# An attention and gMLP kernel on one core: three x transposes moved to DMA, two gMLP batches begun four slots later, four products open in the tail

## The chip, the cores and the metric

The kernel runs on one core of a Trainium2 chip. The metric is the device time of one execution in microseconds; several runs are summed up by their median. A profile is taken of one execution by the hardware profiler.

## The reference

Block-sparse attention for 4 batches of 8 heads (768 positions, head size 64), then a gMLP block with a spatial gate over each batch's attention output. The parts that matter:

```python
scores = scale * np.matmul(q, k.transpose(0, 1, 3, 2))
scores = np.where(mask, scores, -1000000000.0)
attn = np.exp(scores - np.max(scores, axis=-1, keepdims=True))
attn = attn / (np.sum(attn, axis=-1, keepdims=True) + 1e-09)
attn_out = np.matmul(attn, v)
# heads side by side: x is (4, 768, 512)
h = np.maximum(x @ w_in, 0.0)            # 512 -> 1024
u, v = h[..., :512], h[..., 512:]
v_n = (v - mean(v)) / np.sqrt(var(v) + 1e-06)
v_s = np.einsum('ts,bsd->btd', w_spatial, v_n) + b_spatial[None, :, None]
out = (u * v_s) @ w_out
```

Inputs and output are float32; the kernel multiplies in bf16.

## The kernel before

**Pairs and slots.** Two heads of a batch form a pair, so there are 16 pairs, four for each batch: pairs 4 to 7 are batch 1, 8 to 11 batch 2, 12 to 15 batch 3. The program is written as a list of slots, 0 to 188. Each slot emits one piece of the scores (two matmuls, L471) with its exp on ScalarE (L475), and the product with v (six matmuls, L522) of a piece seven slots older. From slot 36 on pair p has twelve slots from `slot_of(p)` = 36 + 12 (p - 4). Every engine takes its instructions in the order in which they are written; only data and buffers decide when.

**Between the pieces** come gMLP steps. A gMLP batch is 108 steps, each one matmul of 512 columns (L596): 48 for v and u (`in_steps`; a product is four steps, one for each pair of the batch, which needs that pair's transposed x), 36 for the spatial product (`s_product`), 24 for the output (`o_product`). Steps wait in one queue. For batch 0 the table `STEPS` says how many run in which slot; batches 1 and 2 are dealt over 48 slots by `deal` and `run_queue`, 2.25 a slot. Batch 3 comes behind the last slot, in the tail. Its start is `last_x` (slot 188): it first empties the queue.

**x of a pair.** When both heads of a pair are normalized by VectorE (L486 and L487; in the 19th slot of the pair, counted from its first as 0: slot 90 for pair 7), x lies with positions on partitions. The gMLP needs it transposed (`xt`). Pairs whose number leaves a remainder of 0 to 2 by four have that done by a DMA transpose from the SP queue (`xtr_dma`, L553). Pairs 7 and 11 have it done on TensorE (`xtr_pe`: six transposes of 128x128, L289, and a copy on VectorE, L218), and pair 15 the same way inside `last_x`. Batches 1 and 2 begin in the slot in which pair 7 and pair 11 are transposed, 92 and 140.

**The SP queue** carries nearly all DMAs in written order: the loads of q, k, v of a pair 34 slots ahead (L110), the DMA transpose of a pair's q and k (`tr_dma`, L428, `tt<-nat`) 20 slots ahead, x transposes (L553), transposes of the gated product (L678) and stores of the output (L697). An issue waits for its data and for the DMA that stands eight places ahead of it in the queue. VectorE later copies `tt` into place (`split`), five and three slots ahead of the pair.

**PSUM.** A product holds a bank until it is copied out. In the loop the gMLP has two banks (`moeA`, `moeB`); in the tail `moe_ps` turns round six. `last_x` before opens three products of batch 3 with the steps of pairs 12 to 14, transposes x of pair 15 in between, and then closes them.

Of the kernel before, what the change touches and what calls it, by code (L numbers as in the profile page):

```python
# [26 lines left out]
def kernel(  # L27
# [18 lines left out]
    B, H, S, D = q.shape  # L46
# [3 lines left out]
    NCH = S // 128  # L50
# [6 lines left out]
    NG = H // 2  # L57
    NP = B * NG
# [6 lines left out]
    TW = TC * 128  # L65
    S0 = NT * NG * 3
# [150 lines left out]
    def dve_copy(o, i):  # L217
        nc.vector.tensor_copy(out=o, in_=i)  # L218
# [58 lines left out]
    moe_tags, held = deque(["moeA", "moeB"]), set()  # L277

    def moe_tag():
        moe_tags.rotate(1)  # L280
        if moe_tags[0] in held:
            moe_tags.rotate(1)
        return moe_tags[0]

    def bank(nm="ps", tag=None):
        return psum.tile([128, 1024], BF16, tag=tag or moe_tag(), bufs=2 if tag else 1, name=nm)

    def tr(ps, c, in_):
        nc.tensor.transpose(out=ps[:, c * 128:(c + 1) * 128], in_=in_, identity=ident)  # L289

    def pair_of(src, c):
        return src[:, c].rearrange("p h d -> p (h d)")
# [142 lines left out]
    a_ref, av_ref, x_ref, xn_ref, xt_ref = {}, {}, {}, {}, {}  # L435
# [96 lines left out]
    def xt_tile(p):  # L532
        if p not in xt_ref:
            xt_ref[p] = work.tile([128, S], BF16, tag="xt", bufs=7, name="xt")
        return xt_ref[p]

    def xtr_pe(p, xn, c0, n, ps=None):
        if ps is None:
            ps = bank()
        for c in range(n):  # L540
            tr(ps, c, pair_of(xn, c))
        dve_copy(xt_tile(p)[:, c0 * 128:(c0 + n) * 128], ps[:, 0:n * 128])
# [180 lines left out]
    def deal(steps, slots):  # L723
        queue.extend(steps)
        pace["slots"], pace["credit"] = slots, 0.0

    def run_queue(n=None):
        if n is not None:
            for _ in range(n):
                queue.popleft()()  # L730
            return
        if not queue or pace["slots"] <= 0:
            return
        pace["credit"] += (len(queue) - pace["credit"]) / pace["slots"]
        pace["slots"] -= 1
        n = int(pace["credit"] + 0.5)
        for _ in range(min(n, len(queue))):
            queue.popleft()()
            pace["credit"] -= 1
# [5 lines left out]
    def when(slot, *fns):  # L745
        at.setdefault(slot, []).extend(fns)

    def c(f, *a, **kw):
        return lambda: f(*a, **kw)
# [19 lines left out]
    def moe_begin(b):  # L769
        moe[b] = Moe(b)  # L770
# [19 lines left out]
    when(18, lambda: first["steps"].popleft()())  # L790
    when(20, close_first)
    when(29, lambda: deal(moe[0].in_steps("v2 v3 u2 u3", TC), 14))
    STEPS = {20: 0, 21: 3, 22: 2, 23: 0, 24: 2, 25: 1, 26: 2, 27: 2, 28: 0, 29: 1, 30: 1, 31: 1, 32: 2, 33: 1, 34: 1, 35: 1, 36: 1, 37: 0, 38: 1, 39: 2, 40: 2, 41: 2, 42: 1, 43: 3, 44: 3, 45: 0, 46: 2, 47: 1, 48: 2, 49: 1, 50: 2, 51: 0, 52: 2, 53: 1, 54: 1, 55: 1, 56: 2, 57: 3, 58: 1, 59: 1, 60: 2, 61: 2, 62: 3, 63: 1, 64: 1, 65: 1, 66: 1, 67: 2, 68: 3, 69: 1, 70: 1, 71: 1, 72: 1, 73: 2, 74: 2, 75: 1, 76: 1, 77: 3, 78: 1, 79: 1, 80: 1, 81: 2, 82: 0, 83: 3, 84: 1, 85: 2, 86: 0, 87: 2, 88: 2, 89: 3, 90: 2, 91: 0}
    when(42, lambda: deal(moe[0].in_steps("v4 v5 u4 u5", TC) + moe[0].rest_steps(),
                          S0 + 8 + 48 - 42))
    for b in (1, 2):
        s0 = S0 + 48 * b + 8
        when(s0, c(moe_begin, b),
             lambda b=b: deal(moe[b].in_steps(SEQ, 3) + moe[b].rest_steps(), 48))

    last_steps = []


    def last_x():
        moe_begin(B - 1)
        m = moe[B - 1]
        while queue:
            queue.popleft()()
        seq = m.in_steps("v0 v1 u0 v2 v3 v4 v5 u1 u2 u3 u4 u5", 3)
        n = NG - 1  # L810
        for i in (0, 1):
            for f in seq[i * NG:i * NG + n]:
                f()
        ps, xn = bank(), xn_ref.pop(("p", NP - 1))
        moe_tags.rotate(1)
        for cc in range(NCH):
            tr(ps, cc, pair_of(xn, cc))
        xt = xt_tile(NP - 1)
        for cs in (slice(0, TW), slice(TW, S)):
            dve_copy(xt[:, cs], ps[:, cs])  # L820
        for f in seq[2 * NG:2 * NG + n]:
            f()
        for i in (0, 1, 2):
            seq[i * NG + n]()
        last_steps.extend(seq[3 * NG:])

    def slot_of(p):
        return S0 + 12 * (p - NG)

    for p in range(NG, NP):  # L830
        g = slot_of(p)
        when({4: 13, 5: 22, 6: 31}.get(p, g - 34), c(load, p, "k"), c(load, p, "q"), c(load, p, "v"))
        when({4: 18, 5: 26, 6: 38}.get(p, g - 24),
             c(cast, p, "k", PL), c(cast, p, "q", PL), c(cast, p, "v", PL))
        when({4: 20, 5: 31}.get(p, g - 20), c(tr_dma, p))
        when(31 if p == 4 else g - (7 if p in (9, 13) else 5), c(split, p, 0))
        when(32 if p == 4 else g - 3, c(split, p, 1))
        if p == NP - 1:
            when(g + 20, last_x)
        elif p % NG == NG - 1:  # L840
            when(g + 20, lambda p=p: xtr_pe(p, xn_ref.pop(("p", p)), 0, NCH))
        else:
            when(g + 20, c(xtr_dma, p))
    for i, (ld, ca) in enumerate([(16, 19), (16, 21), (17, 23), (17, 25), (18, 27), (18, 29)]):
        when(ld, c(ws_load, i))
        when(ca, c(ws_cast, i))
# [12 lines left out]
    for s in range(NS + LAG + 2):  # L859
# [11 lines left out]
        for f in early:  # L871
            f()
        run_queue(STEPS.get(s))
        for f in late.get(s, []):
# [34 lines left out]
```

## Time and profile before

| | |
|---|---|
| median of 3 runs | 209.66 us (209.59 to 211.54) |
| the profiled execution | 209.93 us |
| its span, first to last instruction | 208.1 us |
| mean granted TensorE clock | 0.998 |
| busy: TensorE, weight loads, VectorE, ScalarE, GpSimd | 200.9, 127.8, 133.1, 168.3, 74.3 us |
| DMA | 41.82 MB, 201 GB/s over the span |

The difference between the execution's time and the span lies ahead of the first and behind the last instruction. Times in the timeline are counted from the span's start. Lengths of matmuls overlap: the start of the next one says how long one held the engine.

### The profile page before, as it was taken

Reading aid. Unit: us, or ns where it says so; the run is one execution under the profiler, and the core shown is the slowest. Engines: PE = TensorE matmul, PEld = TensorE weight load, DVE = VectorE, ACT = ScalarE, POOL = GpSimd, SP = SyncE. Lnnn points to the kernel's source line nnn. Section 1 sums busy time; section 2 is a strip of 40 time slices with the busy share of each in tenths; the row PEclk is TensorE's granted clock in tenths of the full one; section 3 lists DMA queues with packets and bytes.
Section 4 is the critical chain, followed back from the end, with each engine's and each line's share of the span. In section 5 each row is a group of like instructions: output and inputs, shape, how many; then the busy total and the mean of one; then the engine's idle time right before and its main releaser. Section 6 shows DMA issues by size and latency. Waiting matters only on the chain.

```text
span 208.1 us, 5248 instructions
## 1 busy us (share of the span) xinstructions
PE 200.9 (96%) x2106; PEld 127.8 (61%) x2140; DVE 133.1 (64%) x287; ACT 168.3 (81%) x223; POOL 74.3 (36%) x116
## 2 busy tenths in 40 slices
PE   8899999999999999999999999999999999999993
PEld 6689778766666666655655565565556556544441
DVE  7578797989764455594986464385885433567542
ACT  6899999999989889989898888979999787266021
POOL 7998789684681404042064040041020000003000
PEclk9999999999999999999999999999999999999999
DMA  5999999999998989899735597896101324610266
GB/s 142 357 365 324 316 405 250 251 282 303 269 336 169 303 222 270 236 305 285 195 124 113 128 242 175 258 244 135 38 3 27 62 54 92 245 57 2 50 150 254
DMA packets 64139, 41.82 MB, mean 201 GB/s; under 512 B 45172, under 2 KB 58868, under 8 KB 64116
## 3 DMA queue, kind: packets, MB, share of 16 engines
q1 hardware_dynamic: 63540, 40.91, 77.0%
q10 hardware_dynamic: 576, 0.59, 0.8%
q8 instruction: 16, 0.26, 0.5%
q14 instruction: 7, 0.06, 0.1%
HBM read 24.38 MB, written 6.29 MB: 147 GB/s over the span
## 4 chain that ended last, share of the span: by engine, by line
PE 85%; ACT 7%; DMA 4%; issue 1%; DVE 1%; SPq 0%; ACTq 0%
PE ps_moe L596 29%; PE ps L471 21%; PE ps_av L522 12%; PE ps_t L596 8%; ACT a_all L463 6%; PE ps L458 5%; PE ps_sc L596 4%; PE ps_av L504 3%; DMA st_q<-in_q_dram 2%; DMA tt<-nat 2%; PE wps L182 1%; PE ps L289 1%; PE ps_av L289 1%; ACT osb L221 0%; ACT a_all L475 0%
## 5 line engine op out<-in xcount | busy, mean ns | idle before, releaser
L475 ACT ACTIVATE a_all<-ps 128x768 bf16<-128x768 f32 x144 | 113.6, 812 | 14.4 <-PE ps L471 8.2
L471 PE MATMUL ps<-kq 88*128 88x384 bf16 x288 | 70.4, 325 | 0.4
L522 PEld LDWEIGHTS <-a_all 128*128 128x128 bf16 x864 | 45.2, 97 | 20.0
L522 PE MATMUL ps_av<-vv,a_all 128*128 128x65 bf16 x864 | 49.8, 193 | 0.0
L471 PEld LDWEIGHTS <-kq 88*128 88x128 bf16 x288 | 27.7, 98 | 29.7
L596 PE MATMUL ps_moe<-w_in_t,xt 128*128 128x512 bf16 x127 | 38.6, 378 | 0.5
L463 ACT ACTIVATE a_all<-ps 128x1024 bf16<-128x1024 f32 x36 | 34.0, 1031 | 1.8 <-PE ps L458 1.5
L596 PE MATMUL ps_moe<-vn,w_spt 128*128 128x512 bf16 x99 | 30.2, 377 | 0.4
L138 POOL CAST nat<-st_k 128x768 bf16<-128x768 f32 (+2 forms) x17 | 13.8, 815 | 39.6 <-DMA st_k<-in_k_dram 39.4
L635 POOL TENSOR_SCALAR std<-mv 128x3 f32<-128x3 f32 (+1 forms) x9 | 2.1, 239 | 62.2 <-DVE mv L632 43.7
L458 PE MATMUL ps<-kq 88*128 88x256 bf16 (+3 forms) x140 | 21.9, 278 | 1.3 <-ACT a_all L463 0.5
L668 DVE SCALAR_TENSOR_TENSOR un<-ps_moe,b_col,un 128x512 bf16<-128x512 f32 x18 | 13.5, 748 | 14.0 <-PE ps_moe L596 11.8
L486 DVE RECIPROCAL rc<-ps_av 128x6 f32<-128x6 f32 (+1 forms) x36 | 6.6, 184 | 24.4 <-PE ps_av L522 22.3
L596 PEld LDWEIGHTS <-xt 128*128 128x128 bf16 x192 | 15.5, 98 | 7.6 <-DVE xt L218 0.2
L596 PE MATMUL ps_moe<-w_out_t,gt 128*128 128x512 bf16 x66 | 19.6, 378 | 0.2
L487 DVE TENSOR_TENSOR xn<-ps_av,rc 128x384 bf16<-128x384 f32 (+1 forms) x36 | 18.5, 513 | 1.2
L218 DVE COPY kq<-tt 64x1536 bf16<-64x1536 bf16 x24 | 17.2, 717 | 0.3
L631 DVE BATCH_NORM_STATS2 stats<-vn 128x6 f32<-128x512 bf16 x24 | 16.4, 684 | 1.3 <-ACT vn L626 0.9
L458 PEld LDWEIGHTS <-kq 88*128 88x128 bf16 (+1 forms) x140 | 12.7, 98 | 5.8 <-DVE kq L218 1.4
L138 POOL CAST nat<-st_q 128x768 bf16<-128x768 f32 (+2 forms) x21 | 14.5, 692 | 2.6 <-DMA st_q<-in_q_dram 2.3
L596 PEld LDWEIGHTS <-w_spt 128*128 128x128 bf16 x144 | 11.6, 98 | 5.6
L188 DVE TENSOR_SCALAR vn<-vn,mv,rstd 128x512 bf16<-128x512 bf16 x24 | 13.1, 578 | 2.6 <-POOL rstd L637 2.6
(83 smaller groups left out, 209.3 us busy)
## 6 DMA issues: line engine op xcount, KB each, us to landing
st_v<-in_v_dram SPq DMA_DIRECT2D x16, 384.0 KB, 6.4
st_k<-in_k_dram SPq DMA_DIRECT2D x15, 384.0 KB, 4.4
out_dram<-osb SPq DMA_DIRECT2D x22, 256.0 KB, 2.9
st_q<-in_q_dram SPq DMA_DIRECT2D x12, 384.0 KB, 5.4
ws_f<-in_moe_w_spatial_dram SPq DMA_DIRECT2D x6, 384.0 KB, 8.0
w_f<-in_moe_w_in_dram SPq DMA_DIRECT2D x8, 256.0 KB, 5.9
w_f<-in_moe_w_out_dram SPq DMA_DIRECT2D x4, 256.0 KB, 3.8
st_q<-in_q_dram SPq DMA_DIRECT2D x6, 128.0 KB, 5.2
```

Source lines behind the costliest of these rows:

```text
L138: eng.tensor_copy(out=dst, in_=src)
L188: nc.vector.tensor_scalar(out=out, in0=in0, scalar1=s1, scalar2=s2, op0=o0, **kw)
L218: nc.vector.tensor_copy(out=o, in_=i)
L458: nc.tensor.matmul(out=ps[:, at:at + n * TW], lhsT=kq[0:kr, h, ci * 128:(ci + 1) * 128], rhs=kq[0:kr, h, qcols(t0, n)], start=True, stop=True)
L463: nc.scalar.activation(out=out, in_=ps, func=AF.Exp, scale=0.125)
L471: nc.tensor.matmul(out=ps[:, hf * 512:hf * 512 + HALF], lhsT=kq[0:KR, j % H, ci * 128:(ci + 1) * 128], rhs=kq[0:KR, j % H, S + hf * HALF:S ...
L475: nc.scalar.activation(out=a_ref["h", j][:, ci, :].rearrange("p (b c) -> p b c", b=2), in_=ps.rearrange("p (b c) -> p b c", b=2)[:, :, 0:H ...
L487: nc.vector.tensor_tensor(out=out, in0=ps[:, :, 0:D], in1=rc[:, 0:n].to_broadcast([128, n, D]), op=ALU.mult)
L522: nc.tensor.matmul(out=av_ref[j][:, qc, 0:VA], lhsT=a_ref["h", j][:, ci, qc * 128:(qc + 1) * 128], rhs=vv[p % NVV][:, h, ci, 0:VA], start= ...
L596: nc.tensor.matmul(out=ref["ps"][:, 0:w], lhsT=lhs(i), rhs=rhs(i), start=(i == 0), stop=(i == n - 1))
L631: nc.vector.bn_stats(out=stats, in_=self.vn[:, tcc, :])
L668: nc.vector.scalar_tensor_tensor(out=self.un[:, tcc, :], in0=ps, scalar=b_col[:, tcc:tcc + 1], in1=self.un[:, tcc, :], op0=ALU.add, op1=AL ...
```

## The change

The x of pairs 7, 11 and 15 is transposed by `xtr_dma`, like the others, one slot after its normalization (`g + 19`; the other pairs keep `g + 20`). Batches 1 and 2 begin in slots 96 and 144 in place of 92 and 140. `STEPS` takes one step from each of slots 57, 62, 68, 77, 83, 87, 88 and 89 and gives two to each of slots 92 to 95. The DMA transposes of q and k of pairs 10 and 14 are issued 16 slots ahead in place of 20, behind the x of pairs 7 and 11 in the SP queue. `last_x` opens four products, three steps each, and closes them with one step each; its transposes and copies are gone. At the end of slot 187 batch 2 has nine steps more in the queue than it had, which `last_x` runs first.

```diff
-    STEPS = {..., 57: 3, ..., 62: 3, ..., 68: 3, ..., 77: 3, ..., 83: 3, ..., 87: 2, 88: 2, 89: 3, 90: 2, 91: 0}
+    STEPS = {..., 57: 2, ..., 62: 2, ..., 68: 2, ..., 77: 2, ..., 83: 2, ..., 87: 1, 88: 1, 89: 2, 90: 2, 91: 0, 92: 2, 93: 2, 94: 2, 95: 2}
...
     for b in (1, 2):
-        s0 = S0 + 48 * b + 8
+        s0 = S0 + 48 * b + 12
...
         seq = m.in_steps("v0 v1 u0 v2 v3 v4 v5 u1 u2 u3 u4 u5", 3)
-        n = NG - 1
-        for i in (0, 1):
+        n, opened = NG - 1, 4
+        for i in range(opened):
             for f in seq[i * NG:i * NG + n]:
                 f()
-        ps, xn = bank(), xn_ref.pop(("p", NP - 1))
-        moe_tags.rotate(1)
-        for cc in range(NCH):
-            tr(ps, cc, pair_of(xn, cc))
-        xt = xt_tile(NP - 1)
-        for cs in (slice(0, TW), slice(TW, S)):
-            dve_copy(xt[:, cs], ps[:, cs])
-        for f in seq[2 * NG:2 * NG + n]:
-            f()
-        for i in (0, 1, 2):
+        for i in range(opened):
             seq[i * NG + n]()
-        last_steps.extend(seq[3 * NG:])
+        last_steps.extend(seq[opened * NG:])
...
-        when({4: 20, 5: 31}.get(p, g - 20), c(tr_dma, p))
+        when({4: 20, 5: 31}.get(p, g - (16 if p in (10, 14) else 20)), c(tr_dma, p))
...
+        when(g + (19 if p % NG == NG - 1 else 20), c(xtr_dma, p))
         if p == NP - 1:
             when(g + 20, last_x)
-        elif p % NG == NG - 1:
-            when(g + 20, lambda p=p: xtr_pe(p, xn_ref.pop(("p", p)), 0, NCH))
-        else:
-            when(g + 20, c(xtr_dma, p))
```

More of the change, by code (lines that the diff above doesn't have):

```diff
@@ L792 @@
     when(29, lambda: deal(moe[0].in_steps("v2 v3 u2 u3", TC), 14))
-    STEPS = {20: 0, 21: 3, 22: 2, 23: 0, 24: 2, 25: 1, 26: 2, 27: 2, 28: 0, 29: 1, 30: 1, 31: 1, 32: 2, 33: 1, 34: 1, 35: 1, 36: 1, 37: 0, 38: 1, 39: 2, 40: 2, 41: 2, 42: 1, 43: 3, 44: 3, 45: 0, 46: 2, 47: 1, 48: 2, 49: 1, 50: 2, 51: 0, 52: 2, 53: 1, 54: 1, 55: 1, 56: 2, 57: 3, 58: 1, 59: 1, 60: 2, 61: 2, 62: 3, 63: 1, 64: 1, 65: 1, 66: 1, 67: 2, 68: 3, 69: 1, 70: 1, 71: 1, 72: 1, 73: 2, 74: 2, 75: 1, 76: 1, 77: 3, 78: 1, 79: 1, 80: 1, 81: 2, 82: 0, 83: 3, 84: 1, 85: 2, 86: 0, 87: 2, 88: 2, 89: 3, 90: 2, 91: 0}
+    STEPS = {20: 0, 21: 3, 22: 2, 23: 0, 24: 2, 25: 1, 26: 2, 27: 2, 28: 0, 29: 1, 30: 1, 31: 1, 32: 2, 33: 1, 34: 1, 35: 1, 36: 1, 37: 0, 38: 1, 39: 2, 40: 2, 41: 2, 42: 1, 43: 3, 44: 3, 45: 0, 46: 2, 47: 1, 48: 2, 49: 1, 50: 2, 51: 0, 52: 2, 53: 1, 54: 1, 55: 1, 56: 2, 57: 2, 58: 1, 59: 1, 60: 2, 61: 2, 62: 2, 63: 1, 64: 1, 65: 1, 66: 1, 67: 2, 68: 2, 69: 1, 70: 1, 71: 1, 72: 1, 73: 2, 74: 2, 75: 1, 76: 1, 77: 2, 78: 1, 79: 1, 80: 1, 81: 2, 82: 0, 83: 2, 84: 1, 85: 2, 86: 0, 87: 1, 88: 1, 89: 2, 90: 2, 91: 0, 92: 2, 93: 2, 94: 2, 95: 2}
     when(42, lambda: deal(moe[0].in_steps("v4 v5 u4 u5", TC) + moe[0].rest_steps(),
```

## The prediction

> **What bounds the kernel now.** I read the page first: the engine totals, the forty slices, the shares of the chain that ended last.
>
> ```profile
> PE 200.9 (96%) x2106; PEld 127.8 (61%) x2140; DVE 133.1 (64%) x287; ACT 168.3 (81%) x223; POOL 74.3 (36%) x116
> ...
> PE   8899999999999999999999999999999999999993
> ...
> PEclk9999999999999999999999999999999999999999
> ...
> PE 85%; ACT 7%; DMA 4%; issue 1%; DVE 1%; SPq 0%; ACTq 0%
> ```
>
> TensorE is busy in every slice, at full granted clock, and carries 85% of the chain. "Busy" can hide short waits, so the second view is TensorE's timeline around slot 92, where pair 7's x is transposed (L289). Columns: start, length, engine, line, operation, count.
>
> ```profile
> 87.29 0.49 PE L471 MATMUL ps<-kq 88*128 88x384 bf16 x2
> 87.62 0.35 PE L522 MATMUL ps_av<-vv,a_all 128*128 128x65 bf16 x6
> 87.80 0.49 PE L289 MATMUL ps<-ident,xn 128*128 128x128 bf16 x6
> 88.13 0.59 PE L596 MATMUL ps_moe<-w_in_t,xt 128*128 128x512 bf16 x2
> 88.57 0.49 PE L471 MATMUL ps<-kq 88*128 88x384 bf16 x2
> 88.89 0.34 PE L522 MATMUL ps_av<-vv,a_all 128*128 128x65 bf16 x6
> 89.08 0.81 PE L596 MATMUL ps_moe<-w_in_t,xt 128*128 128x512 bf16 x3
> 89.72 0.49 PE L471 MATMUL ps<-kq 88*128 88x384 bf16 x2
> ```
>
> Take start to start, not lengths, which overlap. Two score matmuls hold TensorE 0.33 us (87.29 to 87.62), six AV matmuls 0.18 to 0.19, a gMLP step 0.64/3 = 0.215, and the six transposes 87.80 to 88.13 = **0.33**, or 0.055 each. A slot with n steps is 0.51 + 0.215 n. Adding these up from slot 36 meets the later slot starts, 87.29 among them, within 0.05 us, so from about 46 us on TensorE never waits (a gap of 0.21 now and then is one missing record). What leaves its queue leaves the span; what makes it wait enters it.
>
> **The change part by part.**
>
> *The transposes.* Three pairs lose six transposes each on TensorE: 18 x 0.055 = **-0.99 us**, all on the path. VectorE also loses three sets of xt copies (some 0.6 us a pair); it is busy 83 of 134 us in the loop, so they count nothing.
>
> ```profile
> 42.00:176.00 134.00, 132.60 (x1401) 81.53 (x1426) 83.19 (x164) 119.55 (x162) 37.47 (x48) 1.00 0.79 187
> ```
>
> *The moved steps.* Eight steps of batch 0 leave slots 57 to 89 for 92 to 95; batch 2 starts four slots later at 108/48 = 2.25 steps a slot, so nine more of its steps are flushed in slot 188. A step costs 0.215 wherever TensorE is the bound: sum zero. It would cost where ScalarE took over in the thinned slots.
>
> ```profile
> 46.37 2.22 ACT L475 ACTIVATE a_all<-ps 128x768 bf16<-128x768 f32 x3
> 48.92 10.18 ACT L475 ACTIVATE a_all<-ps 128x768 bf16<-128x768 f32 x13 [0.33 <-PE ps L471]
> ...
> 85.91 0.59 ACT L221 ACTIVATE osb<-ps_moe 128x512 f32<-128x512 f32 x1
> ...
> L475 ACT ACTIVATE a_all<-ps 128x768 bf16<-128x768 f32 x144 | 113.6, 812 | 14.4 <-PE ps L471 8.2
> ```
>
> Three exps fit in 2.22 us and the last alone is about 0.81, so a new one starts every (2.22 - 0.81)/2 = 0.70, below even a one-step slot (0.73). In slots 57 to 91, 35 exps need 24.5 us and one output copy 0.6; TensorE after the change needs 35 x 0.513 + 46 x 0.2157 = 27.9. Lower bound 0. Upper bound: each exp holds ScalarE its whole 0.812 (the mean in the last row), 35 x 0.812 + 0.59 = 29.0, a loss of 1.1. I take 0, since the row shows the overlap.
>
> *Pair 7's wait.* Now a transfer has to land before batch 1's first product reaches its fourth step, and every instruction on TensorE queues behind that weight load. Before, x 7 was normalized at 86.78 + 0.56 = 87.34:
>
> ```profile
> 86.55 0.20 DVE L486 RECIPROCAL rc<-ps_av 128x6 f32<-128x6 f32 x1 [1.62 <-PE ps_av L522]
> 86.78 0.56 DVE L487 TENSOR_TENSOR xn<-ps_av,rc 128x384 bf16<-128x384 f32 x1
> 87.25 0.68 DVE L218 COPY osb<-ps_moe 128x512 f32<-128x512 f32 x1
> ```
>
> Eight steps fewer come ahead of it, so 87.34 - 8 x 0.2157 = 85.6. On SP a store of batch 0's output (tile 3) stands ahead of the transfer; its product ends in slot 90, its copy (0.69) follows the normalization, 86.2, its issue takes about 0.5: the transpose is issued at **86.7**. Slot 92 starts at 87.29 - 1.73 = 85.56, slots 92 to 95 have two steps each (4 x 0.943), slot 96 starts at 89.3, and the fourth step is the second of slot 97: 89.33 + 0.94 + 0.51 + 0.22 = **91.0**. The transfer may take 4.3 us.
>
> ```profile
> DMA to landing us min/median/max: 2.7/2.8/5.2
> ...
> tt<-nat SPq DMA_TRANSPOSE x1, 8.1
> xt<-xn SPq DMA_TRANSPOSE x1, 5.2
> ...
> xt<-xn SPq DMA_TRANSPOSE x1, 4.3
> ...
> st_v<-in_v_dram SPq DMA_DIRECT2D x1, 384.0 KB, 5.6
> ```
>
> The first row is all nine xt transfers; the next are those issued at 60.46, behind a tt that took 8.1, and at 81.08; the last a v load issued at 85.79. SP's timeline places them:
>
> ```profile
> 76.73 3.63 SPq L428 DMA_TRANSPOSE tt<-nat  x1
> ...
> 81.08 2.48 SPq L553 DMA_TRANSPOSE xt<-xn  x1
> ...
> 85.79 0.54 SPq L110 DMA_DIRECT2D st_v<-in_v_dram  x1
> 86.42 0.41 SPq L697 DMA_DIRECT2D out_dram<-osb  x1
> 86.93 3.43 SPq L428 DMA_TRANSPOSE tt<-nat  x1
> ```
>
> With the change pair 11's loads are ahead of x 7, issued some 2.5 us earlier than here because their stores come earlier (v at about 83.2, landed by 88.8), and pair 10's tt, at 86.93 here, goes behind x 7 instead of ahead of it. Two stores remain. I take 3.5 us, between the quiet 2.8 and the 4.3 at 81.08: landed by 90.2, stall 0. Bounds 0 and, with 5.2, 0.9.
>
> *Pair 10's and 14's tt.* Pair 10's goes out when x 7's issue is over, 88 to 89.2 (that issue took 2.48 at 81.08). With the longest tt, 8.1, it lands by 96.1 to 97.3; the copy that reads it is in slot 103, at 96.2 by the slot sums. A late copy holds VectorE's queue, where the next gMLP eviction is in slot 106, some 3 us on, and the pair's scores start in slot 108. Price 0, upper bound 0.5. Pair 14's meets fewer loads, the same answer.
>
> *Pair 11.* x was normalized here at 134.50 + 0.56:
>
> ```profile
> 134.50 0.56 DVE L487 TENSOR_TENSOR xn<-ps_av,rc 128x384 bf16<-128x384 f32 x1
> ```
>
> The same reckoning (less 1.73 and pair 7's 0.33, slots of 0.995) gives 133.0 ready, about 133.9 issued behind three stores, needed in slot 145 at 138.9. It may take 5.0, the longest seen is 5.2: stall 0, bound 0.2.
>
> *The tail.*
>
> ```profile
> 179.83 0.34 PE L522 MATMUL ps_av<-vv,a_all 128*128 128x65 bf16 x6
> 180.01 1.03 PE L596 MATMUL ps_moe<-w_out_t,gt 128*128 128x512 bf16 x4
> 180.88 1.46 PE L596 MATMUL ps_t<-w_in_t,xt 128*128 128x512 bf16 x6
> 182.18 0.50 PE L289 MATMUL ps<-ident,xn 128*128 128x128 bf16 x6
> 182.51 0.81 PE L596 MATMUL ps_sc<-w_in_t,xt 128*128 128x512 bf16 x2
> 183.16 0.59 PE L596 MATMUL ps_t<-w_in_t,xt 128*128 128x512 bf16 x2
> ...
> 180.44 0.56 DVE L487 TENSOR_TENSOR xn<-ps_av,rc 128x384 bf16<-128x384 f32 x1
> ```
>
> Before: 4 flushed steps, 6 opening, 6 transposes, 3 opening (one record is missing), and the first closing step at 183.16, with no gap. After, the last AV starts 0.66 + 9 x 0.2157 = 2.6 earlier, 177.2; x 15 is ready at 181.00 - 2.6 = 178.4; a store of batch 2 delays the issue to about 179.0; with the quiet 2.8 it lands at 181.8. TensorE meanwhile has 13 steps of batch 2 and 12 opening ones: 177.4 + 25 x 0.2157 = 182.8. Cover left 1.0; at 5.2 the stall is 1.4. I take 0: loads and tt are over by then.
>
> One new wait I do expect. From the first closing step TensorE had 39 steps to the spatial product; now four products are open, and it has 36, 7.8 us. VectorE's statistics do not get shorter:
>
> ```profile
> 191.12 1.06 DVE L188 TENSOR_SCALAR vn<-vn,mv,rstd 128x512 bf16<-128x512 bf16 x3 [1.09 <-POOL rstd L637]
> ...
> 191.57 2.75 PE L596 MATMUL ps_t<-vn,w_spt 128*128 128x512 bf16 x11
> ```
>
> The last vn is ready at 192.18, 9.0 after 183.16; the spatial product's sixth step would start (36 + 5) x 0.2157 = 8.8 after. **+0.2**. Flushed products that wait for a copied bank: 0 to 0.05 (a copy of 0.68 must fit into the 0.86 of the product between); I take 0.03.
>
> *Sum.* -0.99 + 0.2 + 0.03 = -0.76. The profiled execution took 209.93, so it would take 209.2; the median is 0.27 lower, 209.66, so **208.9**.
>
> **The rivals.**
>
> *x 7 lands late, at 5.2 us* (91.9, stall 0.9): 209.8. For it: three loads and two stores are ahead of it, and the transfer at 60.46 behind a tt took that long. Against: no tt is ahead here. By the Trainium skill (DMA: Bandwidth & Descriptors, Queues, rings and completion order) each DMA engine takes one queue's descriptors in ring order; the 60.46 row agrees, landing just after its tt.
>
> *Slower: x 7 waits like a tt, 8.1 us.* If the backlog of loads is not drained, it lands at 94.8, all of TensorE's queue stands 3.8 us at slot 97: 212.7. It decides from 5.1 us on (4.3 plus the 0.76 gained), and beyond 7.2 it is more than 1% slower. Against: the longest xt of nine is 5.2. The Trainium skill (VectorE: DVE Perf Modes, The three transpose paths) gives 1309 ns by DMA against 390 on TensorE for one block and prefers TensorE; six in turn would be 7.9 us, an estimate from it, landing at 94.6 and 212.5 in all. The rows disagree: six blocks land in 2.7 to 5.2.
>
> *ScalarE becomes the bound in slots 57 to 91*: +1.1, 210.0. Against it the row of three exps.
>
> *The change does more than its transposes*: over 1% faster would need 1.3 us beyond -0.76. No TensorE gap is there to be closed.
>
> **How the numbers follow.** Forecast 0.64; x 7 at 5.2 us or a similar stall at x 15, 0.16; ScalarE 0.05; slower 0.12; faster by over 1% 0.03. One per cent, 2.1 us, is about what a measurement of this kernel can tell from no change. Within it are the first three, 0.85. The range: 208.4 is 0.99 gained plus 0.3 of spread; 210.8 takes in 209.8, 210.0 and a stall of both x 7 and x 15; the long stall is left out.
>
> **What would show it.** Right: L289 with xn sources has 18 fewer instructions, slot starts after 46 us follow the sums, batch 1's first product is not held, a gap of about 0.2 stands before the spatial product's last vn, and span falls by 0.8. Wrong: a weight load of xt waiting for a DMA near 91 or 182, or exps back to back with TensorE waiting for ScalarE between 57 and 86 us.

## The result, and the profile after

| | before | after |
|---|---|---|
| median of 22 runs each, on one chip | 210.1 us | 211.19 us |
| the profiled execution (time, span, mean granted clock) | 209.93, 208.1, 0.998 | 210.91, 209.1, 1.0 |
| the waits of TensorE's matmuls for xt in it | none | 1.0 us in sum |

The changed kernel takes 1.0048 times the time of the kernel before, with a 95% interval of 1.0028 to 1.0068: about 1.0 us slower, where 0.76 faster was forecast. (The ratios leave out executions far above the fastest of their kernel, so they need not equal the quotient of two medians.)

The engine totals, the granted clock and the chain of the changed kernel:

```profile
PE 199.8 (96%) x2087; PEld 126.4 (60%) x2122; DVE 129.4 (62%) x283; ACT 168.0 (80%) x223; POOL 75.6 (36%) x116
...
PEclk9999999999999999999999999999999999999999
...
PE 82%; DMA 7%; ACT 7%; issue 2%; DVE 1%; ACTq 0%
```

TensorE is busy for 1.1 us less (199.8 for 200.9), the clock is full: the work was taken out. (Of the 3.7 us that VectorE is busy for less, 1.8 are the three pairs' copies of xt.) But DMA has 7% of the chain where it had 4%. Three pieces of the chain, in which start and length are those of a DMA from its issue to its landing, say which:

```profile
86.40 4.81 DMA xt<-xn
...
133.89 5.37 DMA xt<-xn
...
179.29 4.46 DMA xt<-xn
```

They are the transposes of x of pairs 7, 11 and 15, all three on the path. The view of waits (engine, line, releaser: us in total, times, longest) from 40 us on has them as the only DMA that a matmul waits for; under PEld stand the weight loads, ahead of those matmuls for xt (the ones for gt hold up no matmul):

```profile
PEld L596 <- DMA xt<-xn: 1.9, 3, 0.8
PEld L596 <- DMA gt<-un: 0.7, 2, 0.4
PE ps_moe L596 <- DMA xt<-xn: 0.7, 2, 0.4
PE ps_t L596 <- DMA xt<-xn: 0.3, 1, 0.3
```

What the path lost is read start to start, in TensorE's timeline, as in the prediction:

```profile
89.05 0.49 PE L471 MATMUL ps<-kq 88*128 88x384 bf16 x2
...
90.51 0.38 PE L596 MATMUL ps_moe<-w_in_t,xt 128*128 128x512 bf16 x1
91.26 0.60 PE L596 MATMUL ps_moe<-w_in_t,xt 128*128 128x512 bf16 x2 [0.38 <-DMA xt<-xn]
...
138.69 0.34 PE L522 MATMUL ps_av<-vv,a_all 128*128 128x65 bf16 x6
139.31 0.61 PE L596 MATMUL ps_moe<-w_in_t,xt 128*128 128x512 bf16 x2 [0.28 <-DMA xt<-xn]
...
182.64 0.81 PE L596 MATMUL ps_t<-w_in_t,xt 128*128 128x512 bf16 x3
183.80 0.60 PE L596 MATMUL ps_t<-w_in_t,xt 128*128 128x512 bf16 x2 [0.35 <-DMA xt<-xn]
...
191.58 2.98 PE L596 MATMUL ps_t<-vn,w_spt 128*128 128x512 bf16 x12
194.39 1.46 PE L596 MATMUL ps_sc<-vn,w_spt 128*128 128x512 bf16 x6
```

One step starts 0.2157 after the one before it. From 90.51 the next was due at 90.73 and came at 91.26: 0.54 lost. Six AV matmuls hold 0.185, so from 138.69 the next step was due at 138.88, 0.43 ahead of 139.31. But one step is unrecorded there (three weight loads of xt stand beside the two matmuls), and it holds 0.21 of that gap, so 0.22 is lost. In the tail three steps from 182.64 put the next at 183.29, and it came at 183.80: 0.51. Twelve steps of the spatial product should hold 12 x 0.2157 = 2.59 from 191.58, and the next product starts 2.81 after it: 0.22, the wait for the statistics. The number in brackets is smaller than the loss each time (0.38, 0.28, 0.35), because it counts from the modelled end of the matmul ahead.

The last store's issue in the kernel before and after (ScalarE's queue):

```profile
205.32 0.35 ACTq L697 DMA_DIRECT2D out_dram<-osb  x1
```

```profile
205.50 0.35 ACTq L697 DMA_DIRECT2D out_dram<-osb  x1
```

One loss the view of waits does not list. In slot 88 the scores start 0.37 after a step that holds 0.2157, so 0.15 is lost:

```profile
81.80 0.38 PE L596 MATMUL ps_moe<-w_out_t,gt 128*128 128x512 bf16 x1
82.17 0.48 PE L471 MATMUL ps<-kq 88*128 88x384 bf16 x2
```

What released them is ScalarE's exp of slot 86, which ended at 82.12. The same gap stands there in every version with the later beginning, and not in the kernel before.

So the ledger closes. Slot 96 starts at 89.05, where the prediction's sums have 89.33. This execution was 0.43 ahead of the kernel before at slot 44 (46.81 for 47.24), by chance: the programs are the same up to there, and the changed kernel of experiment 9 stands at 47.34. It then lost the 0.15. So -0.28 - 0.99 (transposes) + 0.54 + 0.22 + 0.51 (three x) + 0.22 (statistics) = +0.22, and the last store is issued 0.18 later than before. The rest of the span's 1.0, about 0.8, lies behind that store: 208.1 - 205.32 = 2.8 before, 209.1 - 205.50 = 3.6 after. Two things therefore have to be explained: the three late x, and the ending.

### The profile page after: what moved, and what is told of

Same layout as the page of the kernel before. It is cut to its first block, busy times and chain, and to the rows that moved or that the text cites. A ratio compares the mean times of both kernels' runs of the same rounds, so it can differ in the third digit from the quotient of the medians.

```text
span 209.1 us, 5215 instructions
## 1 busy us (share of the span) xinstructions
PE 199.8 (96%) x2087; PEld 126.4 (60%) x2122; DVE 129.4 (62%) x283; ACT 168.0 (80%) x223; POOL 75.6 (36%) x116
## 4 chain that ended last, share of the span: by engine, by line
PE 82%; DMA 7%; ACT 7%; issue 2%; DVE 1%; ACTq 0%
PE ps_moe L596 28%; PE ps L471 21%; PE ps_av L522 12%; DMA xt<-xn 7%; PE ps_t L596 7%; ACT a_all L463 6%; PE ps L458 5%; PE ps_sc L596 3%; PE ps_av L504 3%; PE wps L182 1%; ACT osb L221 1%; PE ps_av L289 1%; PE ps L289 0%; ACT a_all L475 0%; PE mq L296 0%
## 5 line engine op out<-in xcount | busy, mean ns | idle before, releaser
L635 POOL TENSOR_SCALAR std<-mv 128x3 f32<-128x3 f32 (+1 forms) x9 | 2.6, 285 | 65.0 <-DVE mv L632 62.6
L138 POOL CAST nat<-st_q 128x768 bf16<-128x768 f32 (+2 forms) x21 | 15.7, 746 | 3.9 <-DMA st_q<-in_q_dram 3.6
L218 DVE COPY kq<-tt 64x1536 bf16<-64x1536 bf16 x24 | 15.6, 652 | 0.4
L218 DVE COPY osb<-ps_moe 128x512 f32<-128x512 f32 x11 | 7.6, 690 | 13.1 <-PE ps_moe L596 11.8
L188 DVE TENSOR_SCALAR vn<-ps_moe 128x512 bf16<-128x512 f32 x18 | 12.3, 685 | 4.4 <-PE ps_moe L596 4.3
```

Of the source, the lines that this page charges most:

```text
L138: eng.tensor_copy(out=dst, in_=src)
L188: nc.vector.tensor_scalar(out=out, in0=in0, scalar1=s1, scalar2=s2, op0=o0, **kw)
```

## The experiments

Theory A: the later beginning costs nothing; the x transposes are late because of what stands ahead of them on SP. Theory B: the later beginning itself costs, on ScalarE in the thinned slots or in the longer flush. The first four kernels ran on one chip beside the kernel before (median 210.04).

**1. The later beginning alone.** x of 7, 11 and 15 goes back to TensorE, with the tail of before; `s0`, `STEPS` and the later transposes of q and k stay as changed.

```diff
+        if p == NP - 1:
+            when(g + 20, last_x)          # with the transposes of before
+        elif p % NG == NG - 1:
+            when(g + 20, lambda p=p: xtr_pe(p, xn_ref.pop(("p", p)), 0, NCH))
+        else:
+            when(g + 20, c(xtr_dma, p))
-        when(g + (19 if p % NG == NG - 1 else 20), c(xtr_dma, p))
-        if p == NP - 1:
-            when(g + 20, last_x)
```

> The kernel after with the three x transposes and the start of the tail put back on TensorE; only the later start of batches 1 and 2, the moved steps and the later q, k transposes stay. Theory A (the loss is TensorE waiting for the three x transfers, 0.5, 0.2 and 0.5 us in the profile of after): as before, within 0.2 us, and no wait of TensorE after 46 us. Theory B (moving the steps costs: ScalarE becomes the bound in the thinned slots, or the nine flushed steps lengthen the tail): slower than before by about 1 to 2 us, because the 0.99 us of transposes are back and the cost stays.

Measured: 212.55, ratio 1.0105 (1.0063 to 1.0147). Theory A missed by 2.5 us. The view of TensorE's waits from 40 us on has two entries, and the timeline their places:

```profile
PE ps_moe L596 <- DVE osb L218: 1.2, 1, 1.2
PE ps_moe L596 <- DMA gt<-un: 1.2, 1, 1.2
```

```profile
133.90 0.50 PE L289 MATMUL ps<-ident,xn 128*128 128x128 bf16 x6
135.64 0.38 PE L596 MATMUL ps_moe<-w_out_t,gt 128*128 128x512 bf16 x1 [1.25 <-DVE osb L218]
...
181.52 1.90 PE L596 MATMUL ps_moe<-w_out_t,gt 128*128 128x512 bf16 x8 [1.22 <-DMA gt<-un]
```

Start to start they are 1.41 (the transposes end at 134.23) and 1.39 (five steps from 179.05, one unrecorded, put the next at 180.13): 2.8 together, the loss and a little more. Neither is on ScalarE, which costs only the 0.15 of slot 88. The first: batch 1's output products now fall where pair 11 is transposed on TensorE, the six transposes take one of the loop's two gMLP banks, and the next product has to wait until VectorE has copied out the one before. The second: batch 2 is later against the end, and its last transposed gate (`gt`) lands when the flush is already there. So beginning later is not free by itself. In the changed kernel the first wait cannot arise, as no transpose takes a bank; the second does not in the profiled execution: its gt is issued at 175.57, and the flush reaches it at 178.89. Its landing is not in the trace; with the 3.04 that the same transfer took in experiments 13 and 14, or the 3.2 of others in this profile, 0.1 to 0.3 us are left.

**2. Only pair 15 by DMA**, four products open, 7 and 11 on TensorE:

```diff
-            when(g + (19 if p % NG == NG - 1 else 20), c(xtr_dma, p))
+        if p in (7, 11):
+            when(g + 20, lambda p=p: xtr_pe(p, xn_ref.pop(("p", p)), 0, NCH))
+        else:
+            when(g + (19 if p == NP - 1 else 20), c(xtr_dma, p))
```

> The kernel after with x of pairs 7 and 11 put back on TensorE; x of pair 15 stays a DMA, four products open. Theory A: 0.33 us gained for six transposes, 0.5 lost on the wait for x 15 and 0.2 on the statistics: 0.4 us slower than before. Theory B: 1.5 us or more slower than before.

Measured: 212.95, ratio 1.011 (1.0067 to 1.0152). The same two waits, 1.2 and 1.5; none for the x of 15, which landed in 3.6, covered by them. So this run says nothing of x 15 alone, but repeats the first one's two waits.

**3. Only pairs 7 and 11 by DMA**, pair 15 on TensorE in the tail of before:

```diff
+        if p == NP - 1:
+            when(g + 20, last_x)          # with the transposes of before
+        else:
+            when(g + (19 if p % NG == NG - 1 else 20), c(xtr_dma, p))
```

> The kernel after with pair 15 put back on TensorE and the tail as before; x of pairs 7 and 11 stays a DMA. Theory A: 0.66 us gained, 0.54 and 0.22 lost on two waits: 0.1 us slower than before, waits of TensorE only at pairs 7 and 11. Theory B: about 1 us slower than before.

Measured: 210.38, ratio 0.9991 (0.9956 to 1.0025), not to be told from the kernel before; span 208.0. The only wait of a matmul from 40 us on:

```profile
PE ps_moe L596 <- DMA xt<-xn: 0.6, 2, 0.4
```

Twelve transposes bring 0.66, and the two late x take about as much (0.54 and 0.22 in the changed kernel).

**4. The stores behind x.** Output stores emitted in the five slots ahead of the x of 7, 11 and 15 are held and issued right behind it; the pairs' loads stay ahead.

```diff
+                    store = lambda: (...).dma_start(out=..., in_=osb["t"][:, cs])
+                    stores.append(store) if holding else store()
...
+        if p % NG == NG - 1:
+            when(g + 14, hold)
+            when(g + 19, release)
```

> The kernel after, and the output stores that stand right ahead of the three x transposes on SP (two at pair 7, three at pairs 11 and 15) are emitted right behind them. Theory A with the stores as the cause of the late landing: x 7 lands by 90, x 11 by 137.5, x 15 in 2.8 us; no wait for x, 0.99 gained and 0.23 lost on the statistics, 0.7 us faster than before (ratio 0.9965). Theory A with the loads of pairs 11 and 15 as the cause: x 15 is on time, x 7 and x 11 still wait, about 0.1 us faster than before or equal. Theory B: 0.5 to 1 us slower than before, as after.

Measured: 209.59, ratio 0.9978 (0.9946 to 1.0009). But its profiled execution took 211.43, with one wait, at pair 7:

```profile
85.64 0.44 SPq L110 DMA_DIRECT2D st_k<-in_k_dram  x1
86.12 0.70 SPq L110 DMA_DIRECT2D st_q<-in_q_dram  x1
86.87 0.53 SPq L110 DMA_DIRECT2D st_v<-in_v_dram  x1
87.51 1.21 SPq L553 DMA_TRANSPOSE xt<-xn  x1
```

```profile
92.95 0.60 PE L596 MATMUL ps_moe<-w_in_t,xt 128*128 128x512 bf16 x2 [1.91 <-DMA xt<-xn]
```

No store is ahead of x any more, but pair 11's three loads are, the last of them issued 0.6 us ahead (SP ran later in this execution), and x took 5.4: it landed at 92.91, right behind the v load, which landed at 92.14. That pointed at the loads, and the next runs take loads and stores apart. They ran beside the kernel before (median 210.05).

**5. The loads behind x.** Those of pairs 11 and 15 five slots later, the stores ahead as in the changed kernel. The letters A and B stand anew in what was expected here.

```diff
-        when({4: 13, 5: 22, 6: 31}.get(p, g - 34), c(load, p, "k"), c(load, p, "q"), c(load, p, "v"))
+        when({4: 13, 5: 22, 6: 31}.get(p, g - (29 if p in (11, 15) else 34)), c(load, p, "k"), c(load, p, "q"), c(load, p, "v"))
```

> The changed kernel with the loads of pairs 11 and 15 issued five slots later, right behind the x of pairs 7 and 11 instead of ahead of it; the stores of the output stay ahead. Theory A (the output stores that SyncE issues just before an x hold it up; the loads don't): x of 7, 11 and 15 land late as in the changed kernel (4.8, 5.4, 4.5 us), waits of TensorE for xt about 1.2 us in sum, time 210.8 to 211.4. Theory B (the loads hold up x 7): x 7 lands by 3.5 us and its wait of 0.54 goes, those at 11 and 15 stay, time 210.3 to 210.8.

Measured: 210.21, ratio 1.0002 (0.9983 to 1.0021). In the profile x 7 and x 11 landed in 2.8 each, against 4.81 and 5.37, with the stores still ahead of both, and TensorE has no wait for xt. That is neither of the two expectations as written: the loads explain x 11 as well as x 7.

**6. Both behind** (the edits of 4 and 5 together):

> The changed kernel with both the output stores of the five slots ahead of each of the three x and the loads of pairs 11 and 15 issued right behind it. If what stands ahead on SyncE's queue is the whole cause: no wait of TensorE for xt at all in the profile, the three x land in 2.7 to 3.2 us, time 209.2 to 209.6, and the single runs stay within 0.5 us of their median. If SyncE itself runs late (its issue of x 7 after 87): a wait for xt of 0.5 to 1.9 us stays, and the time lies near 209.6 with single runs up to 211.4.

Measured: 209.58, ratio 0.9977 (0.9957 to 0.9996); runs 209.19 to 210.43. No matmul waits for xt; x 7 and x 11 landed in 2.8, but x 15 in 4.5, just in time: without stores ahead it was issued 0.07 us after it was ready, where the changed kernel has 0.48.

**7. Both behind, and batch 2 dealt over 46 slots:**

```diff
-             lambda b=b: deal(moe[b].in_steps(SEQ, 3) + moe[b].rest_steps(), 48))
+             lambda b=b: deal(moe[b].in_steps(SEQ, 3) + moe[b].rest_steps(), 48 if b == 1 else 46))
```

> As the kernel with stores and loads behind x, and the gMLP of batch 2 dealt over 46 slots instead of 48, so that its third transpose gt comes earlier and fewer of its steps are left for the tail. If the third gt of batch 2 is what the later begin endangers (slack 0.1 us in the changed kernel's profile): its slack grows by over 1 us, and the time is that of the kernel without the edit or up to 0.3 lower with less spread. If the flushed steps are the cover that the x of pair 15 needs: a wait for that x of 0.5 to 1.0 us appears in the tail, and the time rises by as much.

Measured: 210.02, ratio 0.9992 (0.9972 to 1.0012), 0.44 above experiment 6. Neither expectation: x 15 landed in 2.8, and the new wait is for a bank, in the flush (whether it makes up the 0.44 is not shown; the profile is of the fastest run):

```profile
179.42 0.81 PE L596 MATMUL ps_moe<-w_out_t,gt 128*128 128x512 bf16 x3 [0.39 <-DVE osb L218]
```

**8. The stores behind, once more** (the kernel of experiment 4):

> The kernel with the output stores behind the three x once more, for a second profile and more single runs. If the late x 7 of its first profile (a wait of 1.91 us) belongs to executions in which SyncE runs late: this profile, if it lies under 210 us, shows no wait for x 7 of more than 0.3 us, and some of the single runs lie again between 210.5 and 211.5. If x 7 is late in all of them because of the loads ahead of it: a wait near 1.9 in this profile too, at a time of 209.6.

Measured: 209.42, ratio 0.9971 (0.9954 to 0.9987). The profiled execution (span 207.9) shows no wait of a matmul for xt. The loads went out earlier this time, and the v load landed ahead of the need of x:

```profile
L110 SPq DMA_DIRECT2D st_v<-in_v_dram x1: 467/467/467, 83.5 to 83.5; - x1
DMA to landing us min/median/max: 4.7/4.7/4.7
...
L553 SPq DMA_TRANSPOSE xt<-xn x1: 1211/1211/1211, 85.8 to 85.8; - x1
DMA to landing us min/median/max: 3.3/3.3/3.3
```

(The first row of each pair has the duration of the issue in ns and its start, the second the time to landing in us.) None of its twelve runs is above 209.84, so the runs near 211 that were expected again did not come. The loads are ahead of x 7 in both executions of this kernel, and both times x landed 0.8 us behind the v load (92.91 behind 92.14, 89.09 behind 88.26). So what decides is when that load lands.

**9 to 11.** The changed kernel again, the kernel of experiment 5 again, and both behind with pair 15 on TensorE in the tail of before; beside the kernel before (median 210.05).

> The changed kernel as it is, beside the next two on one chip. Both theories: 210.9 to 211.4, with a second profile whose waits for xt at pairs 7, 11 and 15 are 0.3 to 0.7 us each (sum 0.8 to 1.6).

> The kernel with only the loads of pairs 11 and 15 behind the x of 7 and 11, once more. Theory L (the three loads in flight, each landing 4 to 5.4 us after its issue, are what x 7 and x 11 wait behind on the queue): x 7 and x 11 land in 2.7 to 3.1 us again and have no wait; what is left over the kernel with stores and loads behind is the x of pair 15, with a wait of 0.2 to 0.6 us in the tail; time 209.9 to 210.3. Theory S (the stores; the quiet landings of its first profile were luck): x 7 or x 11 lands in over 4 us and is waited for by 0.3 us or more.

> Stores and loads behind the x of pairs 7 and 11 as in the kernel with both; pair 15 transposed on TensorE with the tail of before. By the terms of the sum the tail by DMA is worth 0.33 us less 0.2 for the wait for the statistics: so 209.6 to 209.8, 0.1 to 0.2 above the kernel with both, if the x of 15 costs nothing there; the same 209.5 or below it, if that x is still late in part of its executions.

*The changed kernel again:* 210.95, ratio 1.0013 (0.9986 to 1.0041). This sample alone does not tell it from the kernel before; the first, of 22 runs, does. In the profile only x 7 is waited for (landing 4.9); x 11 took 4.7 and x 15 3.8 and both were just in time, so 0.8 to 1.6 expected was too much:

```profile
PE ps_moe L596 <- DMA xt<-xn: 0.5, 1, 0.5
```

*The loads behind, again:* 210.3, ratio 0.9995 (0.9969 to 1.0021). x 7 and x 11 (the two below) landed in 2.8 once more, though on SP four and three stores stand right ahead of them:

```profile
80.06 6.62 SPq L697 DMA_DIRECT2D out_dram<-osb  x4
86.77 1.27 SPq L553 DMA_TRANSPOSE xt<-xn  x1
```

```profile
L553 SPq DMA_TRANSPOSE xt<-xn x1: 1267/1267/1267, 86.8 to 86.8; - x1
DMA to landing us min/median/max: 2.8/2.8/2.8
...
L553 SPq DMA_TRANSPOSE xt<-xn x1: 1255/1255/1255, 133.7 to 133.7; - x1
DMA to landing us min/median/max: 2.8/2.8/2.8
```

Theory L holds for the landings of x 7 and x 11. Its wait for x 15 did not show (3.7, just in time). And the stores themselves say why the loads matter. The two that were issued last ahead of x 7, in the changed kernel and then in this one:

```profile
L697 SPq DMA_DIRECT2D out_dram<-osb x2: 356/384/412, 84.2 to 86.0; - x2
DMA to landing us min/median/max: 5.5/5.5/5.5
```

```profile
L697 SPq DMA_DIRECT2D out_dram<-osb x2: 332/332/332, 84.3 to 86.3; - x2
DMA to landing us min/median/max: 2.0/2.1/2.2
```

Behind the loads a store takes 5.5, without them 2.1. In the changed kernel the v load, issued at 83.60, took 5.4 and so landed at 89.0; x, behind it and two stores, landed at 91.2. Pair 11's x shows the whole queue: its v load landed at 136.30, the three stores at 137.27, 137.89 and 138.54, and x at 139.26.

*Both behind, old tail:* 209.56, ratio 0.9955 (0.9929 to 0.9982), span 207.8, no wait for xt. It does as well as experiment 6, so four open products and the DMA of x 15 bring nothing that can be measured here.

**12 to 14. The ending.** With the loads behind and no wait for xt, the profiled kernel of experiment 10 starts slot 96 at 89.44, 0.11 later than the sums, and issues its last store at 204.56, 0.76 earlier than the kernel before (0.72 when both are counted from their slot 44):

```profile
89.44 0.49 PE L471 MATMUL ps<-kq 88*128 88x384 bf16 x2
```

```profile
204.56 0.35 ACTq L697 DMA_DIRECT2D out_dram<-osb  x1
```

Yet its span is 208.2, as before: 3.6 us lie behind that store, where the kernel before has 2.8, and its time is level. The changed kernel has 3.6 in both of its profiles (205.41 to 209.0 in the second). With the stores behind it is 3.2 to 3.3, with the tail of before 3.1. The trace's records of semaphore waits show what SyncE does there: at the end of the program it waits for the semaphores of all DMAs in a fixed order, two at a time. The kernel before is held up at the third of these waits (until 206.99), the changed kernel at the first (until 207.64), and so has all the others still to go through. The kernel gives its DMAs eight semaphores in turn, and the change adds three DMAs. So three loads were cut in two (five in the second and third of these kernels, with k and q of pair 14), to move the turn alone.

```diff
-        eng.dma_start(out=st[nm, p][:, hs, cs.start * D:cs.stop * D],
-                      in_=dram(SRC[nm], p, hs, cs))
+        for h in (H0, H1) if (nm, p) in (("k", 15), ("q", 15), ("v", 15)) else (hs,):
+            eng.dma_start(out=st[nm, p][:, h, cs.start * D:cs.stop * D],
+                          in_=dram(SRC[nm], p, h, cs))
```

> The kernel before, with the loads of k, q and v of pair 15 each cut into two DMAs of half the size: three DMAs more, as in the changed kernel, and so the last store takes another of the eight DMA semaphores. Theory T (the time from the last store's issue to the span's end hangs on which of the eight semaphores the last store has, since SyncE waits for them in a fixed order at the end): 3.3 to 3.6 us there instead of 2.8, and the time 0.4 to 0.8 above the kernel before. Theory C (it belongs to the changed kernel's code or tail): 2.8, and the time within 0.2 of the kernel before.

> The kernel with the loads behind x 7 and x 11, with the loads of pair 15 and k and q of pair 14 each cut into two DMAs: five more, with the three of the change eight, so that the last store takes the same semaphore as in the kernel before. Theory T: 2.8 to 3.0 us from the last store's issue to the span's end instead of 3.6, and a time of 209.4 to 209.7 instead of 210.2 to 210.3. Theory C: 3.6 and 210.2 to 210.4.

> Stores and loads behind x, with the same five loads cut in two. Theory T: 2.8 to 3.0 us behind the last store's issue instead of 3.2, and a time of 209.1 to 209.4 instead of 209.58. Theory C: 3.2 and 209.5 to 209.7.

Measured, beside the kernel before (median 209.95): the kernel before with three more DMAs 210.29, ratio 1.0025 (1.0 to 1.0049); the loads behind with five more 209.96, ratio 0.9996 (0.9981 to 1.0011); both behind with five more 209.56, ratio 0.9978 (0.9964 to 0.9992). The last stores, in this order, with spans of 209.0, 208.0 and 208.2:

```profile
205.72 0.35 ACTq L698 DMA_DIRECT2D out_dram<-osb  x1
```

```profile
204.57 0.36 ACTq L698 DMA_DIRECT2D out_dram<-osb  x1
```

```profile
205.04 0.35 ACTq L708 DMA_DIRECT2D out_dram<-osb  x1
```

That is 3.3, 3.4 and 3.1 behind them. In the semaphore records the wait that is held up is the first in the first kernel and the third in the two others, as theory T has it. Its sizes are not borne out. The kernel before has 0.4 more there and 0.34 in the median, so theory C falls, as far as one profile of each and an interval that begins at 1.0 can tell. But the others have only 0.2 and 0.1 less, and 0.3 and 0 in the median.

The landing of the last store splits this time in two (us):

| kernel | store issued to landed | landed to the end |
|---|---|---|
| before | 1.97 | 0.86 |
| changed | 2.12 | 1.49 |
| before, three more (12) | 2.11 | 1.16 |
| loads behind (10) | 2.11 | 1.50 |
| loads behind, five more (13) | 2.57 | 0.86 |
| both behind (6) | 2.11 | 1.13 |
| both behind, five more (14) | 2.29 | 0.84 |

Behind the landing, then, the turn of the semaphores does what theory T says: 0.30 more in experiment 12, and back to the kernel before in 13 and 14. What theory T leaves out is that the store itself landed later there, by 0.5 and 0.2. Of the changed kernel's 0.8, some 0.3 is the turn, 0.15 the landing, and 0.3 a pause of 0.35 between the last two waits (207.86 to 208.21), which experiments 6 and 12 do not have; what makes that pause stays open.

| kernel | x 7, 11, 15 landed in | waits for xt | behind the last store | median | ratio |
|---|---|---|---|---|---|
| changed | 4.8, 5.4, 4.5 | 1.0 | 3.6 | 211.19 | 1.0048 |
| changed, again (9) | 4.9, 4.7, 3.8 | 0.5 | 3.6 | 210.95 | 1.0013 |
| stores behind (4) | 5.4, 3.6, 3.9 | 1.9 | 3.3 | 209.59 | 0.9978 |
| stores behind (8) | 3.3, 3.5, 3.7 | 0 | 3.3 | 209.42 | 0.9971 |
| loads behind (5) | 2.8, 2.8, 3.7 | 0 | 3.6 | 210.21 | 1.0002 |
| loads behind (10) | 2.8, 2.8, 3.7 | 0 | 3.6 | 210.3 | 0.9995 |
| both behind (6) | 2.8, 2.8, 4.5 | 0 | 3.2 | 209.58 | 0.9977 |
| both, old tail (11) | 2.7, 2.8, - | 0 | 3.1 | 209.56 | 0.9955 |

The versions of experiments 4 (and 8), 6, 11 and 14 beat both kernels, by 0.39 to 0.63 us in the median against the one before, 0.2 to 0.3%; only the first interval of experiment 4 includes 1. What they have over the loads behind alone lies at the end: from slot 44 to the last store's issue experiments 5, 6, 8, 10, 11 and 14 all take 157.4 to 157.5 us (158.08 in the kernel before).

## Why the prediction was wrong

**The step that failed is the landing of the three x.** The prediction took 3.5 us for x 7, up to 5.0 for x 11 and the quiet 2.8 for x 15; they took 4.81, 5.37 and 4.46. The other terms of those steps were right: x 7 was forecast to be issued at 86.7 and needed at 91.0 (86.40, and due at 90.73, in an execution that is 0.28 ahead of the sums at slot 96), x 11 to be issued at 133.9 (133.89). So three stalls stood at 0 that came to 0.54, 0.22 and 0.51 in the profiled execution, 1.27 in all, more than the 0.99 from the transposes. Each lay within its own bound or at it (0.9, 0.2, 1.4); together they had no price. The range was said to take in a stall of both x 7 and x 15, but by these bounds that is 208.9 + 0.9 + 1.4 = 211.2, above its end of 210.8.

**Why it failed for x 7 and x 11.** The prediction named the loads that stand ahead and judged them landed by 88.8; the v load landed at 89.0. It then treated the transfer as nearly quiet, while x lay in the queue behind those loads and behind two stores that had been held up by them. With the loads behind x it lands in 2.7 to 2.8, in every one of seven profiles. With them ahead it takes 3.3 to 3.6 where no store stands between and the loads are early, 5.4 where they are late, and 4.7 to 5.4 with stores between: it lands 0.6 to 0.8 behind the last load, 2.2 behind it with two stores between and 2.6 to 3.0 with three. From the prediction's own 88.8 that is 91.0, and nothing is left of the cover. The Trainium skill (DMA: Bandwidth & Descriptors, Queues, rings and completion order) says that an engine takes one queue's descriptors in ring order; the runs agree (a store takes 5.5 behind the loads, 2.1 without them). The rule was cited for the rival and not used for the forecast's own transfer.

**x 15.** No load is ahead there. It took 3.6 to 4.5 in ten of eleven profiles and 2.8 only where batch 2 ran faster, so the quiet value was the exception. Taking away the stores did not quicken it (4.5, 3.7, 3.9, 3.6 in experiments 6, 8, 4 and 14), but lets it be issued 0.4 sooner after it is ready. What slows it stays open. The DMA packets show a candidate that no run moved: the fetch of 16 KB of instructions (queue q8 of the page). In nine of those ten profiles one begins 0.6 to 1.1 us after the issue of x 15, and x takes longer with it: 3.7 with a fetch of 0.97 (experiment 8), 4.5 with 1.58 and 1.71 (the changed kernel, experiment 6). In the run with 2.8 it had begun before the issue. Experiment 2 does not fit (it too began before, and x took 3.6). No fetch falls into x 7, and into x 11 only shorter ones (0.3 to 0.6), some of them beside landings of 2.8.

**The ending** was in no step. With x on time the path did about what the sum said: 0.72 less from slot 44 to the last store's issue in experiments 5 and 10, for 0.76 forecast (the parts measured here, -0.99, 0.22 and the 0.15 of slot 88, make 0.62; 0.1 stays unexplained). The 0.8 more behind that store took it back (both are level with the kernel before). The late x then made level into slower. Whether a kernel comes out above or below the one before hangs on both: late x and the long ending, +1.0 us; x on time with the long ending, +0.16 and +0.25; with the stores behind as well, -0.39 to -0.63.

**The rivals.** The late x 7 had the right mechanism and place; its price of 0.9 was for x 7 alone, and the 0.16 was for x 7 or x 15. That the same shortfall strikes three transfers at once, all put behind a batch's stores on one queue, was not a case of its own. The rival with 8.1 us did not come: the longest of these three in any profile is 5.4. ScalarE as the bound came in one slot: 0.15 in slot 88, with the later beginning alone too. The prediction put this at nothing because 35 exps of 0.70 fit into TensorE's 27.9 us of slots 57 to 91; but the comparison holds slot by slot. Slots 86 to 88 have no step, one and one after the change and hold TensorE 0.51, 0.73 and 0.73, so the exps fall behind there and cannot use the room of fuller slots.

**What was right.** -0.99 for the transposes, by the path above. +0.2 for the statistics: 0.22. Nothing for the moved steps: right but for those 0.15, and narrowly. What the prediction did not see there is the third gt of batch 2, whose slack shrank to 0.1 to 0.3 us, and the bank for which the output products would have waited had the transposes stayed on TensorE (experiment 1). The range, 208.4 to 210.8, missed the median by 0.4. That distance owes something to chance: the forecast starts from 209.66, the median of three runs of the kernel before, which 22 runs put at 210.1. The change itself was forecast at -0.76 and measured at about +1.0.

## What to carry to other kernels

Price a transfer that joins a queue by the landing of the last load ahead of it and the transfers between (here about 0.7 for each store and 0.6 to 0.8 for x), not by a middle of landings seen elsewhere. Compare two engines slot by slot, not by their totals. Work that is moved from the bounding engine to a queue pays only if the order of that queue is moved with it: the same transposes come out 1.0 us slower with loads and stores ahead, and 0.4 to 0.6 faster with these behind (0.3 to 0.5 of that difference lies behind the last store). A batch that is begun later uses up margins far away (a bank, the last transposed gate), so try that shift by itself.

## What the runs showed that was not expected

The time behind the last store's issue is not the same for all versions: 2.8 us before, 3.1 to 3.6 in the others, as much difference as the sum that was forecast. Cutting three loads of the kernel before in two, with nothing else changed, made it 0.4 longer in the one profile taken; the DMAs take eight semaphores in turn, and the end of the program waits for them in a fixed order.

Single executions also shift against each other by more than the margins of the change: x 7 was issued between 85.28 and 87.71 in these profiles. A transfer with 0.5 us of slack is on time in one execution and late in the next. Whether late x also makes the runs spread is not shown: the versions with x on time keep their twelve runs within 0.75 to 1.24 us (experiments 5 to 8, 10, 11 and 14), but the kernel before, without these transfers, spreads over 2.1 (209.4 to 211.54).
